# Linear attention feeding a top-1 mixture of experts on one core: a head pair per load, tiles of two token chunks, and weight casts four pieces behind their loads

## The chip, the cores and the metric

The kernel runs on one core of a Trainium2 chip. The metric is the device time of one execution in microseconds. The kernel before was run three times: 467.87, 472.14 and 472.62 us, median 472.14. The profiled execution took 468.79 us.

In profiles PE is TensorE (PEld its weight load), DVE is VectorE, ACT is ScalarE, POOL is GpSimd and SP is the sync engine, which here only issues loads. Each engine works its own instructions off in order.

## The reference

```
q, k, v: (8 batches, 8 heads, 576 tokens, 64) float32
kv  = einsum('bhsd,bhse->bhde', k, v)
out = einsum('bhsd,bhde->bhse', q, kv)
rms = sqrt(mean(out * out, axis=-1) + 1e-6)
x   = (out / rms * g_norm)  as (4608 tokens, 512)
logits = x @ w_gate                       # 8 experts
e      = argmax(logits);  gate = softmax(logits)[e]
y      = gate * (relu(x @ w1[e]) @ w2[e]) # w1: 512x1024, w2: 1024x512, float32
```

Inputs are 28.3 MB of q, k and v, and 33.6 MB of expert weights.

## The kernel before

**Attention stage.** Batches are taken in pairs j (two batches r = 0, 1), and within a pair four head pairs i. A *tile* is one of q, k or v for one (j, i): 128 partitions by 18 runs of 64, 590 KB. Partitions 0 to 63 hold batch r = 0, partitions 64 to 127 batch r = 1, and each half is loaded by a DMA of its own (L186, two DMAs of 64 partitions for a tile, issued by SP). A partition holds nine neighbouring tokens of two heads, so each contiguous run in HBM is 2304 bytes. There are four buffers for k, four for v and three for q.

For each tile triple, `kv_slice` (L218) accumulates k and v products in PSUM, nine chunks of tokens, in 64x64 quarters of the array. `t_slice` (L202) transposes q, and ACT copies the result (L206). After four head pairs `fold` (L237) multiplies kv by an identity and by the gate weights, so that the attention output and the logits come from one product. `o_tile` (L262) then makes 128 tokens for all heads: matmuls into PSUM, ACT squares (L270), DVE sums (L274), ACT takes the root (L276, L277), DVE scales into `xrow` (L279) and into `lhat` (L283). Two PSUM buffers alternate. Nine o_tiles make one j. `route` computes the expert, the gate and each token's slot, and POOL scatters each o_tile's rows to a table `x_slots` in HBM (L343), nine scatters in a row for j = 0, 1, 2 and three times three for j = 3.

**Weights.** A *piece* is 512 KB: one quarter of w1 (L163) or w2 (L167) of one expert, numbered 0 to 63 here. SP loads it into one of three float32 buffers `wst`, and a cast (L172) writes it to float16 and frees the buffer. Pieces 0 to 23 are interleaved with the attention loads, two for each tile triple, and cast on POOL. The others are cast on DVE.

**Expert stage.** For each of eight experts POOL gathers 640 rows (L405), PE transposes them (L424), DVE copies (L425), PE multiplies by w1 (L443), ACT applies relu (L451), PE multiplies by w2 (L455), DVE scales (L460) and POOL scatters to the output (L463). One more tile of 128 rows serves an expert with more than 640 tokens; its weights are gathered by POOL (L548, L554).

The order of the instructions on an engine is set by a scheduler when the kernel is built: it starts from program order and moves instructions where it expects their operands early. So casts stand in DVE's order far from where the program names them.

Of the kernel before, what the change touches and what calls it, by code (L numbers as in the profile page):

```python
# [11 lines left out]
F32 = mybir.dt.float32  # L12
F16 = mybir.dt.float16
# [9 lines left out]
B, H, S, DH = 8, 8, 576, 64  # L23
# [19 lines left out]
def kernel(  # L43
# [30 lines left out]
    for j in range(4):  # L74
        for t in range(9):
            tok[:, j, t] = (2 * j + ar // 64) * S + 9 * (ar % 64) + t

# [8 lines left out]
        "pcol": arf[:, None],  # L86
        "w1off": arf[:, None] + 128.0 * np.arange(4, dtype=np.float32)[None, :],
        "w2off": arf[:, None] + 128.0 * np.arange(8, dtype=np.float32)[None, :],
# [34 lines left out]
    wgt = P_const.tile([128, 4, 8], F32, tag="wgt")  # L123
    nc.scalar.dma_start(wgt, moe_w_gate.rearrange("(t p) j -> p t j", p=128))
    epsb = P_const.tile([128, 1], F32, tag="epsb")
# [28 lines left out]

    def w_chunk(e, n, pool, bufs, cast):
        if n == 0:
            w_tiles[e] = (
                pool.tile([128, 4, F], F16, tag="w1e", bufs=bufs, name=f"w1e{e}"),
                pool.tile([128, 8, D], F16, tag="w2e", bufs=bufs, name=f"w2e{e}"),
            )  # L160
        st = P_wa.tile([128, F], F32, tag="wst", bufs=3, name=f"wst{e}_{n}")
        if n < 4:
            nc.sync.dma_start(st, moe_w1[e, 128 * n : 128 * n + 128, :])  # L163
            dst = w_tiles[e][0][:, n, :]
        else:
            m = 2 * (n - 4)
            nc.sync.dma_start(  # L167
                st.rearrange("p (t d) -> p t d", t=2),
                moe_w2[e, 128 * m : 128 * m + 256, :].rearrange("(t p) d -> p t d", p=128),
            )  # L170
            dst = w_tiles[e][1][:, m : m + 2, :].rearrange("p t d -> p (t d)")
        cast(dst, st)  # L172

    with (
# [4 lines left out]

        def load_pair(j, i):  # L180
            for n, src in (("k", k), ("v", v), ("q", q)):
                t = PA.tile(
                    [128, 18, 64], F32, tag=f"m{n}", bufs=3 if n == "q" else 4, name=f"m{n}{j}{i}"
                )
                for r in range(2):
                    nc.sync.dma_start(  # L186
                        t[64 * r : 64 * r + 64].rearrange("p (h c) d -> p h (c d)", h=2),
                        src[2 * j + r, 2 * i : 2 * i + 2].rearrange("h (p c) d -> p h (c d)", c=9),
                    )
                main[n, j, i] = t  # L190

        qT, kvps, kvx = {}, {}, {}

        def t_slice(j, i):
            if i == 0:
                qT[j] = PA.tile([128, 36, 128], F32, tag="qT", bufs=2, name=f"qT{j}")
            src = main["q", j, i].rearrange("p b d -> p (b d)")
            for u in range(3):
                ps = PSA.tile([128, 3, 128], F32, tag="T", bufs=2)
                for c in range(3):  # L200
                    m = 3 * u + c
# [3 lines left out]
                m = 9 * i + 3 * u  # L205
                nc.scalar.copy(qT[j][:, m : m + 3, :], ps)  # L206

        def kv_slice(j, i):
            if i == 0:
                kvps[j] = [  # L210
                    PSA.tile([128, 4, 64], F32, tag=f"KV{r}", bufs=1, name=f"kvps{j}{r}")
                    for r in range(2)
                ]
            for c in range(9):
                for a in range(2):
                    for r in range(2):
                        rs_ = slice(64 * r, 64 * r + 64)
                        nc.tensor.matmul(  # L218
                            kvps[j][r][64 * a : 64 * a + 64, i, :],
                            main["v", j, i][rs_, 9 * a + c, :],  # L220
                            main["k", j, i][rs_, 9 * a + c, :],
                            start=(c == 0), stop=(c == 8),
                        )

        def fold(j):
            for r in range(2):
                z = PA.tile([128, 4, 64], F32, tag="z", bufs=2)
                nc.vector.tensor_copy(z, kvps[j][r])
                x = PA.tile([128, 4, 2, 72], F32, tag="kvx", bufs=4, name=f"kvx{j}{r}")
                pss = [  # L230
                    PSA.tile([128, 4, 72], F32, tag="T", bufs=2, name=f"fold{a}") for a in range(2)
                ]
                for i in range(4):
                    for a in range(2):
                        hs = slice(64 * a, 64 * a + 64)
                        for d in range(2):
                            nc.tensor.matmul(  # L237
                                pss[a][64 * d : 64 * d + 64, i, :], z[hs, i, :], fold_r[hs, i, :],
                                start=True, stop=True,
                            )  # L240
                for a in range(2):
                    nc.vector.tensor_copy(x[:, :, a, :], pss[a])
                kvx[2 * j + r] = x

        xrow, lhat = {}, {}

        def o_tile(j, t):
# [7 lines left out]
            ps = PSA.tile([128, 2, 512], F32, tag="O", bufs=2)  # L255
            for i in range(4):
                for a in range(2):
                    blk = 9 * (2 * i + a) + t
                    hs = slice(64 * (blk % 2), 64 * (blk % 2) + 64)
                    for r in range(2):  # L260
                        rs_ = slice(64 * r, 64 * r + 64)
                        nc.tensor.matmul(  # L262
                            ps[rs_, a, 72 * i : 72 * i + 72],
                            qT[j][hs, blk // 2, rs_],
                            kvx[2 * j + r][hs, i, a, :],
                            start=True, stop=True,
                        )
            pv = ps[:, :, 0:288].rearrange("p a (h c) -> p a h c", c=72)
# [10 lines left out]
            nc.vector.tensor_tensor(  # L279
                xr[:, 0:D].bitcast(F16).rearrange("p (h a d) -> p a h d", a=2, h=4),  # L280
                pv[:, :, :, 0:64], _bc(rs2, 3, 64), op=ALU.mult,
# [67 lines left out]

        w_order = [(e, n) for e in range(3) for n in range(8)]  # L350

        def w_some(n):
            for _ in range(min(n, len(w_order))):
                e, c = w_order.pop(0)
                w_chunk(e, c, P_wa, 3, nc.gpsimd.tensor_copy)

        for i in range(4):
            load_pair(0, i)
        o_of = {0: (0, 1), 1: (2, 3), 2: (4, 5), 3: (6, 7, 8)}
        for j in range(5):  # L360
            for i in range(4):
                if j < 4:
                    kv_slice(j, i)
                    t_slice(j, i)
                if j + 1 < 4:
                    load_pair(j + 1, i)
                w_some(2)
                if j > 0:
                    for t in o_of[i]:
                        o_tile(j - 1, t)  # L370
                        for t0, t1 in chunks[j - 1]:
                            if t + 1 == t1:
                                route(j - 1, t0, t1)
            if j < 4:
                fold(j)
        w_some(24)

    with (
# [41 lines left out]
        def xpose(xl, xsT, K):  # L420
            for k in range(K):
# [5 lines left out]
                )  # L427

        def ffn(K, xl, idv, w, views, tag=""):
            w1e, w2e = w  # L430
# [5 lines left out]
            for f in range(8):  # L436
# [127 lines left out]

        for n in range(8):
            w_chunk(3, n, PF, 3, nc.vector.tensor_copy)
        for e in range(E):
            if e + 1 < E:
                load_x(e + 1)
            slot_ids(e)  # L570
            if e == 1:
                tabs = dyn_tables()
            if 4 <= e + 3 < E:
                for n in range(8):
                    w_chunk(e + 3, n, PF if e + 3 < 6 else P_wa, 3, nc.vector.tensor_copy)
# [42 lines left out]
```

## Time and profile before

| | value |
|---|---|
| median of three runs | 472.14 us |
| profiled execution | 468.79 us |
| its span (first to last instruction) | 467.0 us |
| mean granted PE clock, share of full | 0.779 |
| PE, DVE, ACT, POOL busy | 68%, 36%, 24%, 35% of the span |
| moved by DMA | 83.80 MB, mean 179 GB/s |

Three parts follow each other: attention with loads (to about 180 us), attention's last tiles and routing (to 234 us), and the experts. A share of busy time over the whole span says little, since each part waits for something else. Read the stretches apart. The granted clock is that of PE: 0.50 is 1.2 GHz, 1.00 is 2.4 GHz.

### The profile page before, as it was taken

The numbers are of one execution on the slowest core, as the hardware profiler recorded it, in microseconds if no ns is written. First come the engines' busy times: TensorE is split into PE (matmuls) and PEld (weight loads), VectorE is DVE, ScalarE is ACT, GpSimd is POOL, SyncE is SP. The second block draws the span as 40 slices with busy tenths as digits, with TensorE's granted clock in tenths as the row PEclk, the third lists the DMA queues.
The fourth block names the chain that finished last, engine by engine and source line by source line (L and its number), as shares of the span: only waits on it lengthen the run. The fifth ranks groups of instructions, "written<-read, shape, count | busy, mean of one in ns | idle before, by whom it ended". The sixth has DMA issues, their size and how long they took to land. (4 is left out here: it accounts for less than half of the span.)

```text
span 467.0 us, 9241 instructions
## 1 busy us (share of the span) xinstructions
PE 315.7 (68%) x3782; PEld 221.1 (47%) x3782; DVE 166.5 (36%) x415; ACT 113.3 (24%) x299; POOL 163.2 (35%) x161
## 2 busy tenths in 40 slices
PE   2677766757675879343027965893759696969891
PEld 2576655656564667233014543361425354545550
DVE  2001624226322455266356634633302223232311
ACT  1211522115220345042102222040022131323330
POOL 3001111551107410714272450743753525252212
PEclk9999556557566568855556999796958999999997
DMA  8999999999999895301166897879461313131101
GB/s 200 241 243 264 255 253 246 269 268 237 231 217 245 231 266 183 124 25 54 49 209 210 292 349 257 313 267 268 128 95 56 102 34 113 36 131 45 62 34 74
DMA packets 37003, 83.80 MB, mean 179 GB/s; under 512 B 5981, under 2 KB 7262, under 8 KB 36960
## 3 DMA queue, kind: packets, MB, share of 16 engines
q1 hardware_dynamic: 27136, 61.88, 50.0%
q0 software_dynamic: 8704, 21.06, 14.8%
q8 instruction: 30, 0.49, 0.5%
q10 hardware_dynamic: 1120, 0.27, 0.3%
q14 instruction: 13, 0.11, 0.1%
HBM read 71.75 MB, written 15.50 MB: 187 GB/s over the span
## 5 line engine op out<-in xcount | busy, mean ns | idle before, releaser
L451 ACT ACTIVATE hT<-hp 128x320 f16<-128x320 f32 (+1 forms) x136 | 51.4, 427 | 172.1 <-PE hp L443 107.1
L443 PE MATMUL hp<-xsT,w1e 128*128 128x320 f16 x512 | 81.4, 315 | 15.9 <-ACT hT L451 10.3
L455 PE MATMUL yp<-w2e,hT 128*128 128x512 f16 x320 | 77.0, 400 | 15.8 <-DVE y L460 13.2
L262 PE MATMUL ps<-kvx,qT 64*64 64x72 f32 x1152 | 51.3, 307 | 41.5 <-DVE lhat L283 26.7
L463 POOL DMA_INDIRECT out_dram<-y,idv x41 | 42.5, 1036 | 98.8 <-DVE y L460 87.6
L218 PE MATMUL kvps<-mk,mv 64*64 64x64 f32 x1152 | 56.0, 292 | 28.2 <-issue 15.2
L443 PEld LDWEIGHTS <-w1e 128*128 128x128 f16 x512 | 52.0, 102 | 42.0 <-issue 20.7
L218 PEld LDWEIGHTS kvps<-mk,mv 64*64 64x64 f32 x1152 | 51.9, 197 | 31.5 <-issue 31.4
L262 PEld LDWEIGHTS ps<-kvx,qT 64*64 64x64 f32 x1152 | 41.7, 197 | 48.9 <-issue 43.7
L455 PEld LDWEIGHTS <-hT 128*128 128x128 f16 x328 | 33.3, 102 | 57.8 <-issue 21.1
L460 DVE TENSOR_SCALAR y<-yp,xl 128x512 f32<-128x512 f32 x41 | 30.7, 749 | 74.5 <-PE yp L455 72.6
L343 POOL DMA_INDIRECT x_slots<-xrow,posi x36 | 34.9, 970 | 53.3 <-DVE posi L327 23.7
L274 DVE TENSOR_REDUCE ms<-sq 128x8 f32<-128x512 f32 x36 | 24.6, 685 | 70.8 <-ACT sq L270 48.4
L405 POOL DMA_INDIRECT xl<-x_slots,xidx x40 | 42.7, 1068 | 14.8 <-issue 11.3
L270 ACT ACTIVATE sq<-ps 128x512 f32<-128x512 f32 x36 | 21.4, 597 | 96.0 <-PE ps L262 64.9
L202 PE MATMUL ps<-ctile,mq 128*128 128x128 f32 x144 | 34.8, 399 | 2.8 <-ACT qT L206 1.4
L206 ACT COPY qT<-ps 128x384 f32<-128x384 f32 x48 | 22.6, 478 | 49.0 <-PE ps L202 48.5
L424 PE MATMUL ps<-h,xl 128*128 128x128 f16 x164 | 16.2, 231 | 25.1 <-DMA xl<-x_slots,xidx 15.8
L172 POOL CAST w2e<-wst 128x1024 f16<-128x1024 f32 x12 | 12.5, 1044 | 57.2 <-DMA wst<-in_moe_w_dram 57.2
L172 POOL CAST w1e<-wst 128x1024 f16<-128x1024 f32 x12 | 12.3, 1042 | 56.0 <-DMA wst<-in_moe_w_dram 56.0
L202 PEld LDWEIGHTS ps<-ctile,mq 128*128 128x128 f32 x144 | 24.1, 202 | 9.9 <-ACT qT L206 6.3
L279 DVE TENSOR_TENSOR xrow<-ps,rs 128x512 f16<-128x512 f32 x36 | 24.7, 685 | 8.1 <-ACT rs L277 8.0
(86 smaller groups left out, 187.7 us busy)
## 6 DMA issues: line engine op xcount, KB each, us to landing
wst<-in_moe_w_dram SPq DMA_DIRECT2D x64, 512.0 KB
mk<-in_k_dram SPq DMA_DIRECT2D x32, 288.0 KB
mv<-in_v_dram SPq DMA_DIRECT2D x32, 288.0 KB
mq<-in_q_dram SPq DMA_DIRECT2D x32, 288.0 KB
out_dram<-y,idv POOLq DMA_INDIRECT x41
xl<-x_slots,xidx POOLq DMA_INDIRECT x40
x_slots<-xrow,posi POOLq DMA_INDIRECT x36
ctile<-c_all ACTq DMA_DIRECT2D x1, 133.0 KB
```

Of the source, the lines that this page charges most:

```text
L172: cast(dst, st)
L202: nc.tensor.transpose(ps[:, c, :], src[:, 128 * m : 128 * m + 128], cv["ident"])
L218: nc.tensor.matmul(kvps[j][r][64 * a : 64 * a + 64, i, :], main["v", j, i][rs_, 9 * a + c, :], main["k", j, i][rs_, 9 * a + c, :], start=( ...
L262: nc.tensor.matmul(ps[rs_, a, 72 * i : 72 * i + 72], qT[j][hs, blk // 2, rs_], kvx[2 * j + r][hs, i, a, :], start=True, stop=True,)
L279: nc.vector.tensor_tensor(xr[:, 0:D].bitcast(F16).rearrange("p (h a d) -> p a h d", a=2, h=4), pv[:, :, :, 0:64], _bc(rs2, 3, 64), op=ALU. ...
L343: nc.gpsimd.indirect_dma_start(out=xs_views[9 * j + t0 + t], out_offset=IndirectOffsetOnAxis(ap=posi[:, t : t + 1], axis=0), in_=xrow[j, ( ...
L405: nc.gpsimd.indirect_dma_start(out=xl[:, k, :], out_offset=None, in_=xs.ap(), in_offset=IndirectOffsetOnAxis(ap=xidx[:, e, k : k + 1], axi ...
L443: nc.tensor.matmul(hp[a], w1e[:, kk, f * 128 : (f + 1) * 128], xsT[:, kk, s : s + step], start=(kk == 0), stop=(kk == 3),)
L451: nc.scalar.activation(hT[:, f, s : s + step], hp[a], ACTF.Relu)
L455: nc.tensor.matmul(yp, hT[:, f, k * 128 : (k + 1) * 128], w2e[:, f, :], start=(f == 0), stop=(f == 7),)
L460: nc.vector.tensor_scalar(y, yp, xl[:, k, D : D + 2].bitcast(F32), None, op0=ALU.mult)
L463: nc.gpsimd.indirect_dma_start(out=views[k], out_offset=IndirectOffsetOnAxis(ap=idv[:, k : k + 1], axis=0), in_=y, in_offset=None, bounds_ ...
```

## The change

A tile is now one batch b and a half u of its heads: two head pairs, each of which fills the 128 partitions (head a = 0 on partitions 0 to 63, head a = 1 on 64 to 127). It still has 590 KB and runs of 2304 bytes, but one DMA of 128 partitions loads it (L203). There are still 16 triples, now by (b, u), with the same number of buffers. The fold is done for each batch. An o_tile takes 64 + 64 tokens from two token chunks of one batch; only t = 4 joins the last chunks of the two batches. The row's head order changes to (a, h), and the tables `w1off`, the gate weights' load and the w1 pieces' rows are permuted to match.

A piece is loaded by `w_load` into one of four buffers, and `w_cast` casts the piece that was loaded four pieces earlier. In attention `w_step` does one piece for each triple from b = 1 on, instead of two. The remaining pieces are named inside the experts' loop over f.

```diff
@@ weights
-        st = P_wa.tile([128, F], F32, tag="wst", bufs=3, name=f"wst{e}_{n}")
+        st = P_wa.tile([128, F], F32, tag="wst", bufs=4, name=f"wst{e}_{n}")
         if n < 4:
-            nc.sync.dma_start(st, moe_w1[e, 128 * n : 128 * n + 128, :])
+            r0 = 128 * (2 * (n % 2) + n // 2)
+            nc.sync.dma_start(st, moe_w1[e, r0 : r0 + 128, :])
...
-        cast(dst, st)
+        w_staged.append((dst, st))
+
+    def w_cast(engine):
+        if w_staged:
+            engine.tensor_copy(*w_staged.pop(0))
@@ loads
-        def load_pair(j, i):
+        def load(b, u):
             for n, src in (("k", k), ("v", v), ("q", q)):
                 t = PA.tile(
-                    [128, 18, 64], F32, tag=f"m{n}", bufs=3 if n == "q" else 4, name=f"m{n}{j}{i}"
+                    [128, 2, 576], F32, tag=f"m{n}", bufs=3 if n == "q" else 4, name=f"m{n}{b}{u}"
                 )
-                for r in range(2):
-                    nc.sync.dma_start(
-                        t[64 * r : 64 * r + 64].rearrange("p (h c) d -> p h (c d)", h=2),
-                        src[2 * j + r, 2 * i : 2 * i + 2].rearrange("h (p c) d -> p h (c d)", c=9),
-                    )
+                nc.sync.dma_start(
+                    t,
+                    src[b, 4 * u : 4 * u + 4].rearrange("(i a) (p c) d -> (a p) i (c d)", a=2, c=9),
+                )
@@ order of the program
-        for j in range(5):
-            for i in range(4):
-                if j < 4:
-                    kv_slice(j, i)
-                    t_slice(j, i)
-                if j + 1 < 4:
-                    load_pair(j + 1, i)
-                w_some(2)
-                if j > 0:
-                    for t in o_of[i]:
-                        o_tile(j - 1, t)
...
-            if j < 4:
-                fold(j)
-        w_some(24)
+        def w_step(n=1):
+            for _ in range(n):
+                if len(w_staged) == 4:
+                    w_cast(nc.gpsimd)
+                w_load(P_wa, 3)
+
+        for b in range(B + 1):
+            j = (b - 1) // 2
+            for u in range(2):
+                if b < B:
+                    kv_slice(b, u)
+                    t_slice(b, u)
+                if b + 2 < B:
+                    load(b + 2, u)
+                if b > 0:
+                    w_step()
+                    for i in (2 * u, 2 * u + 1):
+                        t = 5 * ((b - 1) % 2) + i
+                        o_tile(j, t)
...
+            if b < B:
+                fold(b)
+                if b % 2 == 1:
+                    j = b // 2
+                    o_tile(j, 4)
@@ in ffn, after each f
+                if not tag:
+                    w_cast(nc.vector)
+                    w_next()
```

The first place is SP's queue around the last attention loads (names: `mk33` is k of j = 3, i = 3; `mk71` is k of b = 7, u = 1; `wst2_4` is piece 4 of expert 2). Before:

```order
L163 DMA wst2_2_1251<-in_moe_w1_dram 128x1024
L163 DMA wst2_3_1254<-in_moe_w1_dram 128x1024
L186 DMA mk32_1361<-in_k_dram 64x2x576 x2
L186 DMA mv32_1364<-in_v_dram 64x2x576 x2
L186 DMA mq32_1367<-in_q_dram 64x2x576 x2
L167 DMA wst2_4_1370<-in_moe_w2_dram 128x2x512
L167 DMA wst2_5_1373<-in_moe_w2_dram 128x2x512
L186 DMA mk33_1479<-in_k_dram 64x2x576 x2
L186 DMA mv33_1482<-in_v_dram 64x2x576 x2
L186 DMA mq33_1485<-in_q_dram 64x2x576 x2
L167 DMA wst2_6_1488<-in_moe_w2_dram 128x2x512
```

and now:

```order
L203 DMA mk70_1497<-in_k_dram 128x2x576
L203 DMA mv70_1499<-in_v_dram 128x2x576
L203 DMA mq70_1501<-in_q_dram 128x2x576
L177 DMA wst1_0_1506<-in_moe_w1_dram 128x1024
L203 DMA mk71_1613<-in_k_dram 128x2x576
L203 DMA mv71_1615<-in_v_dram 128x2x576
L203 DMA mq71_1617<-in_q_dram 128x2x576
L177 DMA wst1_1_1620<-in_moe_w1_dram 128x1024
L177 DMA wst1_2_1780<-in_moe_w1_dram 128x1024
L177 DMA wst1_3_1887<-in_moe_w1_dram 128x1024
```

Ahead of the last q tile stood 22 pieces (to piece 5 of expert 2); now nine do (to piece 0 of expert 1), and each tile is one row where two DMAs were.

The second place is DVE's queue where the routing of j = 2 ends and the last batch's o_tiles begin (`kvx` is the folded product that o_tile uses). Before:

```order
L327 CAST posi_2144<-pos_2142 128x9
L242 COPY kvx30_2168<-fold0_2169 128x4x72
L242 COPY kvx30_2168<-fold1_2170 128x4x72
L242 COPY kvx31_2191<-fold0_2192 128x4x72
L242 COPY kvx31_2191<-fold1_2193 128x4x72
L274 TENSOR_REDUCE ms_2233<-sq_2231 128x8
L274 TENSOR_REDUCE ms_2259<-sq_2257 128x8
L279 TENSOR_TENSOR xrow30_2213<-ps_2214,rs_2235 128x2x4x64
```

and now:

```order
L262 COPY kvx6_1995<-fold0_1996 128x2x144
L352 CAST posi_1970<-pos_1968 128x9
L262 COPY kvx6_1995<-fold1_1997 128x2x144
L190 CAST w2e1_1505<-wst1_4_2071 128x1024
L190 CAST w2e1_1505<-wst1_5_2179 128x1024
L299 TENSOR_REDUCE ms_2094<-sq_2092 128x8
L190 CAST w2e1_1505<-wst1_6_2320 128x1024
L299 TENSOR_REDUCE ms_2120<-sq_2118 128x8
L304 TENSOR_TENSOR xrow30_2074<-ps_2075,rs_2096 128x512
```

Before, no cast stood on DVE ahead of the last route; now twelve do (pieces 12 to 23), between the last o_tiles. POOL casts pieces 0 to 11. In the experts' part 25 casts stood ahead of the first y of the second expert, and 27 stand there now.

## Rows read from the trace of the kernel before

**Rows 1.** Busy time by stretch: stretch, length, busy of five engines, clock, DMA share, GB/s.

```profile
50.00:75.00 25.00, 17.08 (x374) 15.53 (x367) 11.98 (x29) 9.15 (x26) 4.17 (x4) 0.50 1.06 253
200.00:225.00 25.00, 9.45 (x232) 8.42 (x233) 16.22 (x56) 9.20 (x28) 5.91 (x7) 0.50 0.11 38
```

**Rows 2.** The same view, three short stretches.

```profile
14.00:18.00 4.00, 2.70 (x56) 2.56 (x58) 0.00 (x0) 0.48 (x1) 0.00 (x0) 1.00 1.06 240
94.00:98.00 4.00, 1.74 (x12) 0.88 (x11) 0.48 (x1) 0.60 (x1) 3.08 (x5) 0.50 1.03 347
300.00:304.00 4.00, 2.92 (x30) 1.88 (x28) 3.46 (x8) 0.44 (x1) 3.17 (x3) 1.00 1.02 396
```

**Rows 3.** Timeline of SP's queue: start, length, engine, line, operation, tile, count.

```profile
33.63 1.61 SPq L163 DMA_DIRECT2D wst<-in_moe_w_dram  x2
...
43.09 3.23 SPq L163 DMA_DIRECT2D wst<-in_moe_w_dram  x2
...
166.26 1.68 SPq L186 DMA_DIRECT2D mq<-in_q_dram  x2
...
251.39 6.13 SPq L163 DMA_DIRECT2D wst<-in_moe_w_dram  x4
...
312.26 5.93 SPq L167 DMA_DIRECT2D wst<-in_moe_w_dram  x4
```

**Rows 4.** Timeline of POOL and ACT around scatters; brackets: idle before, and releaser.

```profile
143.76 0.98 POOL L343 DMA_INDIRECT x_slots<-xrow,posi  x1 [0.17 <-issue]
...
152.64 0.96 POOL L343 DMA_INDIRECT x_slots<-xrow,posi  x1 [0.30 <-issue]
...
155.25 1.10 ACT L270 ACTIVATE sq<-ps 128x512 f32<-128x512 f32 x2 [14.88 <-remote]
```

**Rows 5.** Timeline of POOL, end of routing: the first gather of the experts' rows.

```profile
234.32 1.44 POOL L405 DMA_INDIRECT xl<-x_slots,xidx  x1 [2.83 <-DVE w1e L172]
```

**Rows 6.** Timeline of PE, four kinds of work at 1.2 GHz, and the first matmuls.

```profile
7.80 3.45 PE L218 MATMUL kvps<-mk,mv 64*64 64x64 f32 x72 [7.80 <-DMA mv<-in_v_dram]
...
37.29 1.70 PE L237 MATMUL fold<-fold_r,z 64*64 64x72 f32 x32
...
126.22 3.31 PE L218 MATMUL kvps<-mk,mv 64*64 64x64 f32 x72
...
176.50 2.37 PE L202 MATMUL ps<-ctile,mq 128*128 128x128 f32 x9
...
202.47 2.20 PE L262 MATMUL ps<-kvx,qT 64*64 64x72 f32 x64 [9.81 <-DVE lhat L283]
```

**Rows 7.** Timeline of PE, the same work at 2.4 GHz.

```profile
183.02 1.90 PE L218 MATMUL kvps<-mk,mv 64*64 64x64 f32 x72
184.85 0.87 PE L202 MATMUL ps<-ctile,mq 128*128 128x128 f32 x6
185.97 0.55 PE L202 MATMUL ps<-ctile,mq 128*128 128x128 f32 x3 [0.24 <-ACT qT L206]
...
187.08 0.92 PE L237 MATMUL fold<-fold_r,z 64*64 64x72 f32 x32 [0.29 <-ACT qT L206]
...
190.03 1.32 PE L262 MATMUL ps<-kvx,qT 64*64 64x72 f32 x48 [0.38 <-DVE kvx L242]
```

**Rows 8.** Groups by line: casts on DVE, busy us and mean ns.

```profile
L172 DVE CAST w2e<-wst 128x1024 f16<-128x1024 f32 x20 | 14.0, 701 | 17.3 <-DMA wst<-in_moe_w_dram 15.6 <-issue 1.7
```

**Rows 9.** Timeline of POOL's gathers in the experts' stage.

```profile
299.79 1.25 POOL L405 DMA_INDIRECT xl<-x_slots,xidx  x1 [0.31 <-issue]
301.35 1.02 POOL L463 DMA_INDIRECT out_dram<-y,idv  x1 [0.30 <-DVE y L460]
```

**Rows 10.** Who waited for whom: us in total, times, longest.

```profile
PE yp L455 <- DVE y L460: 13.2, 3, 7.7
```

**Rows 11.** Timeline of POOL: the first casts of pieces.

```profile
43.12 1.04 POOL L172 CAST w1e<-wst 128x1024 f16<-128x1024 f32 x1 [37.95 <-DMA wst<-in_moe_w_dram]
...
55.52 1.04 POOL L172 CAST w1e<-wst 128x1024 f16<-128x1024 f32 x1 [8.51 <-DMA wst<-in_moe_w_dram]
```

More of the change, by code (lines that the diff above doesn't have):

```diff
@@ L123 @@
     wgt = P_const.tile([128, 4, 8], F32, tag="wgt")
-    nc.scalar.dma_start(wgt, moe_w_gate.rearrange("(t p) j -> p t j", p=128))
+    wg_src = moe_w_gate.rearrange("(x y z e) j -> y e x z j", x=2, y=2, z=2)
+    for y in range(2):
+        for x in range(2):
+            nc.scalar.dma_start(wgt[64 * y : 64 * y + 64, 2 * x : 2 * x + 2, :], wg_src[y, :, x])
     epsb = P_const.tile([128, 1], F32, tag="epsb")
@@ L153, with w_load @@
     w_tiles = {}
-    def w_chunk(e, n, pool, bufs, cast):
+    w_todo = [(e, n) for e in range(E) for n in range(8)]
+    w_staged = []
+    def w_load(pool, bufs):
+        if not w_todo:
+            return
+        e, n = w_todo.pop(0)
         if n == 0:
@@ L204, in t_slice, with kv_slice @@
                     )
[L205 to L212, printed above, removed]
+                m = 9 * u + 3 * g
+                nc.scalar.copy(qT[b][:, m : m + 3, :], ps)
+        def kv_slice(b, u):
+            if u == 0:
+                kvps[b] = [
+                    PSA.tile([128, 2, 64], F32, tag=f"KV{a}", bufs=1, name=f"kvps{b}{a}")
+                    for a in range(2)
@@ L213, in kv_slice @@
                 ]
             for c in range(9):
-                for a in range(2):
-                    for r in range(2):
-                        rs_ = slice(64 * r, 64 * r + 64)
+                cs = slice(64 * c, 64 * c + 64)
+                for y in range(2):
+                    for a in range(2):
+                        hs = slice(64 * a, 64 * a + 64)
                         nc.tensor.matmul(
-                            kvps[j][r][64 * a : 64 * a + 64, i, :],
-                            main["v", j, i][rs_, 9 * a + c, :],
-                            main["k", j, i][rs_, 9 * a + c, :],
+                            kvps[b][a][64 * y : 64 * y + 64, u, :],
+                            main["v", b, u][hs, y, cs],
+                            main["k", b, u][hs, y, cs],
@@ L222, in kv_slice, with fold @@
                             start=(c == 0), stop=(c == 8),
                         )
[L225 to L232, printed above, removed]
-                for i in range(4):
-                    for a in range(2):
-                        hs = slice(64 * a, 64 * a + 64)
+        def fold(b):
+            z = PA.tile([128, 2, 2, 64], F32, tag="z", bufs=2)
+            for a in range(2):
+                nc.vector.tensor_copy(z[:, a], kvps[b][a])
+            x = PA.tile([128, 2, 2, 2, 72], F32, tag="kvx", bufs=4, name=f"kvx{b}")
+            pss = [
+                PSA.tile([128, 2, 2, 72], F32, tag="T", bufs=2, name=f"fold{y}") for y in range(2)
+            ]
+            for u in range(2):
+                for a in range(2):
+                    for y in range(2):
+                        ys = slice(64 * y, 64 * y + 64)
@@ L243, in fold @@
-                kvx[2 * j + r] = x
+            for y in range(2):
+                nc.vector.tensor_copy(x[:, :, y], pss[y])
+            kvx[b] = x
         xrow, lhat = {}, {}
```

84 lines of the change are left out of this document (44 added, 40 removed).

## The prediction

> **What bounds the kernel now.** I read the busy time by stretch first, since the three parts have different limits. In the attention part the DMA engines are full (share 1.06) and PE works 17.1 of 25 us at 1.2 GHz; in 200 to 225 us the same engines move 38 GB/s and DVE, with 16.2 of 25 us, is the busiest [rows 1]. So the first part waits for transfers, and the second for a chain of small steps. The three short stretches then show that a full queue does not always move the same: one with attention loads alone moves 240 GB/s, one with weight pieces 347, one with pieces, gathers and output rows 396 [rows 2]. The attention loads are the 64-partition DMAs; the pieces fill 128 partitions.
>
> SP's queue gives the end of the first part: the last q tile is issued at 166.3 us [rows 3]. Until then 47 of the 48 tiles (27.7 MB), 22 pieces of 0.524 MB (11.5 MB) and 18 scatters of 128 rows of 1032 bytes (2.4 MB) have been issued: 41.6 MB in 165.5 us, or 251 GB/s. The first gather of the experts comes at 234.3 us [rows 5], 68 us after that issue, and the span ends at 467.0, 232.7 us later. These three lengths (166.3, 68.0, 232.7) are my terms.
>
> **First term: until the last q tile is issued.** The order shows nine pieces ahead of it where 22 stood, so 34.8 MB remain. At 251 GB/s this takes 139 us; at the 347 of the pieces 100; at 396, 88. The new tile has runs of 2304 bytes in 128 partitions, two to a partition; the w2 pieces have runs of 2048 bytes, two to a partition, also 128 partitions, and they were among what moved at 396 [rows 2]. The run length before is the same 2304 bytes, so what differs is the half of the partitions, and I take 347 rather than 251. The Trainium skill (SBUF — State Buffer, Door 1: The DMA port swizzle) says that partitions 0 to 63 reach only eight of sixteen ports, with asymptotes of 218 and 436 GB/s for half and all, and that two half transfers don't add up. The trace agrees in direction, with 240 beside 347, though 240 is above the page's half. As an estimate from that page, 34.8 MB at 436 GB/s would be 80 us, which leaves the sum as it is, because PE comes next.
>
> For what is late next is PE. The last q tile waits for a buffer, that is for the transposes of tile (6, 0). By the order PE has then done 13.2 kv tiles, 13 transposed tiles, six folds and 23 o_tiles. At 1.2 GHz one costs 3.31, 2.37, 1.70 and 1.10 us (half of the row's two o_tiles) [rows 6]: 43.7 + 30.8 + 10.2 + 25.3 = 110 us. At 2.4 GHz it is 1.90, 1.67 (from 184.85 to the end of the second row), 0.92 and 0.88 us (two thirds of the row) [rows 7]: 25.1 + 21.7 + 5.5 + 20.2 = 72.5 us. To both I add the start, 7.8 us [rows 6], and two scatter blocks: while POOL issues nine scatters PE nearly stops, and ACT goes on at 155.25, after the last of them [rows 4]. From 143.76 that is 11.5 us, of which PE works about 2; two times 9.5 is 19 us. Before, full queues covered these blocks; with faster loads they are bare. PE's path is then 137 us at the low clock and 99 at the high one. The clock rose between 176.5 and 183.0 us [rows 6, 7], where kv tiles and transposes followed each other almost without a wait, so denser work should raise it part of the time. Between 100 (loads) or 99 (PE, high) and 137 (PE, low) I take the middle, **120 us**; the range keeps 100 and 139.
>
> **Second term: from there to the first gather.** The work left is the same as before: three kv tiles and transposes, two folds, 13 o_tiles, four routes and 18 scatters. New are twelve casts on DVE, 0.70 us each [rows 8], 8.4 us in all. DVE had 8.8 us idle in the 25 of [rows 1] and the other half of this part is no denser, so I count them at nothing; the whole 8.4 if that idle time is only waiting inside the chain. Their pieces, 9 to 23, are 7.9 MB, 23 us at 347 GB/s within 68 us in which the queue was nearly empty. POOL is slower beside a cast: a gather took 1.25 us where 1.02 is usual [rows 9]; 0.23 for 18 scatters is 4.1 us at most. The Trainium skill (SBUF — State Buffer, Who interferes with whom) speaks against this move: a DVE copy or cast in a two-port mode and GpSimd lock each other out for a whole instruction. By that rule twelve scatters could each wait 0.70 us, 8.4 us together instead of 4.1; the row shows a third of it. In the other direction the last tile lands sooner: a load took 9.5 us to its cast in a full queue [rows 3, 11], and 251/347 of that saves 2.6. So **68 us**, from 65 to 80.
>
> **Third term: the experts.** SP issues the last 32 pieces in 66.8 us [rows 3], 2.09 us each. Four buffers instead of three let one more be under way, and PE's waits for y that stood behind casts, 13.2 us [rows 10], could go entirely. But the order puts two more casts ahead of the second expert's first y, 4.2 us at 2.09. Between -13.2 and +4.2 I take -5, near the middle: **227.7 us**. The number of pieces left for this part is the same (36 or 37), so there is no bill for those that left the first part: they go into the empty stretch.
>
> **Edits at nothing:** the gate weights' load in four DMAs on ACT's queue, wanted by the first fold only at 37 us; 16 half-sized copies of kvps for eight whole ones; the permuted tables; 48 load issues instead of 96 on SP, which isn't the bound.
>
> **The sum** is 120 + 68 + 227.7 = 415.7 us of span; with the 1.8 us that the execution's 468.8 lies above its span, **418 us**. That execution is 3.3 us below the median of the runs and within their spread, so I leave it at that.
>
> **The rivals.**
> - *The first part keeps its pace.* Either half-partition DMAs weren't the cause of 240, or PE stays at 1.2 GHz: 139 or 137 us lead to the same. For it: PE was at 1.2 GHz through most of this part, and the chain of an o_tile (ACT, DVE, ACT, DVE) leaves it gaps. Against it: the 347. Time: 138 + 68 + 227.7 + 1.8 = 436 us. Chance 0.22.
> - *Everything gives.* PE reaches 2.4 GHz early, loads set 100 us, and the experts' waits for y vanish: 100 + 68 + 219.5 + 1.8 = 389 us. For it: at 183 us one tile triple passed in 3.5 us. Against it: dense work needs loads ahead of it, and scatters break it. Chance 0.12.
> - *Slower: the hand-over of buffers on DVE.* A piece is issued only when the cast four places earlier has run, and these casts now stand between the last o_tiles. If each group of four costs a whole trip from issue to cast, three trips lengthen the second term, and nine (36 pieces) replace the 83.9 us from the first gather to SP's last piece (318.2) [rows 3, 5]. The time is 120 + 68 + 3x + (232.7 - 83.9) + 9x + 1.8. With the second trip in the rows, 43.09 to 55.52, x is 12.4 [rows 3, 11] and the time 487; with the first, 9.5, it is 453. It decides against the change from x = 11.2 on. Against it: both trips ran in a full queue of other loads, which isn't there later. Chance 0.05.
>
> **How the numbers follow.** My forecast, 405 to 430 us with 418 in it, has 0.58; the named rivals 0.39, and 0.03 is left for what I don't see. The range goes from 388 to 450: it takes in the fast rival, the slow pace with the second term's upper bound of 80 (448), and leaves out the hand-over. About 1% is what a measurement of this kernel can tell from no change. Faster by more: forecast, both rivals of the first part and most of the rest, 0.92. Within 1%, 0.03. Slower, 0.05.
>
> **What would show it.** The stretch of attention loads alone at 300 GB/s or more, where 240 stood, shows the first step; a value near 245 refutes it. SP's last q issue near 120 us shows the first term, and the granted clock there (above 0.5 in part of the stretches) the reason for its middle. The first gather 68 us later shows that casts on DVE are covered; waits of DVE's sums or of casts for pieces before the last route would show that they are not. PE's waits for y below 13 us show the third term. I would be wrong most if PE, not the queue, had been setting the first part's pace, or if DVE stood still at pieces in the middle of the last routes.

## The result, and the profile after

The changed kernel takes 428.8 us (median of four runs, 425.4 to 434.0), the kernel before on the same chip 470.0 (464.9 to 472.6). The ratio is 0.917, 95% interval 0.902 to 0.932. Medians and ranges here and below are of all runs of a kernel, while a ratio leaves out runs that lie over 1.5% above the fastest of their kernel. The profiled execution took 425.42 us with a span of 423.6. Forecast were 418 us and a range of 388 to 450.

Busy time by stretch of the changed kernel (columns as in [rows 1, 2]: stretch, length, busy of PE, PE's weight loads, DVE, ACT, POOL, granted clock, DMA share, GB/s):

```profile
14.00:18.00 4.00, 4.00 (x81) 3.48 (x80) 0.49 (x2) 0.95 (x2) 0.00 (x0) 1.00 1.03 380
...
34.00:38.00 4.00, 1.91 (x60) 1.64 (x57) 2.02 (x7) 0.30 (x2) 0.00 (x0) 0.79 1.04 410
...
50.00:75.00 25.00, 15.76 (x281) 11.82 (x281) 7.89 (x30) 4.93 (x15) 10.86 (x11) 0.62 0.64 229
...
102.00:110.00 8.00, 4.43 (x63) 2.96 (x61) 0.69 (x1) 1.08 (x2) 6.17 (x7) 0.71 0.81 253
...
175.00:200.00 25.00, 2.12 (x52) 1.72 (x47) 11.34 (x46) 2.99 (x11) 10.54 (x10) 0.50 0.28 94
```

Read the first row beside that of [rows 2]: the same kind of stretch, attention loads alone and a full queue, moves 380 GB/s where it moved 240, and 410 at 34 us. The third row answers to the first of [rows 1]: from 50 us on the queue is no longer full, 0.64 where 1.06 stood. So the wait for transfers has gone from most of the first part, and something else sets its pace. SP's own waits (engine, line, for whom: us in total, times, longest) name it: the loads wait for the transposes that free the buffers of q.

```profile
SPq L203 <- PE ps L219: 62.2, 10, 12.4
```

The fourth row of the stretches shows one thing that holds PE up: in 8 us in which POOL issues seven scatters, DVE completes one operation and PE 63 matmuls.

The same block on the timelines of POOL, PE, DVE and SP (start, length, engine, line, operation, tile, count; in brackets the idle time before, and who ended it):

```profile
99.17 0.98 POOL L368 DMA_INDIRECT x_slots<-xrow,posi  x1 [8.47 <-DVE posi L352]
...
104.78 0.34 PE L287 MATMUL ps<-kvx,qT 64*64 64x72 f32 x3 [0.85 <-issue]
106.21 0.30 PE L287 MATMUL ps<-kvx,qT 64*64 64x72 f32 x3 [1.08 <-issue]
...
108.31 0.69 DVE L299 TENSOR_REDUCE ms<-sq 128x8 f32<-128x512 f32 x1 [8.96 <-issue]
...
109.33 0.96 POOL L368 DMA_INDIRECT x_slots<-xrow,posi  x1 [0.30 <-issue]
...
123.61 0.37 SPq L203 DMA_DIRECT2D mq<-in_q_dram  x1
...
194.19 1.56 POOL L433 DMA_INDIRECT xl<-x_slots,xidx  x1 [3.18 <-DVE d_gt L520]
```

"Issue" is a wait for nothing that the profile shows. PE gets a few matmuls done between scatters (three at 104.78, three at 106.21), DVE stands for 8.96 us. The last two rows give the lengths: the last q tile at 123.6 us (166.3 in [rows 3]), the first gather at 194.2 (234.3 in [rows 5]), the end at 423.6.

| | before | forecast | after |
|---|---|---|---|
| to the last q's issue | 166.3 | 120 | 123.6 |
| from there to the first gather | 68.0 | 68 | 70.6 |
| from there to the end | 232.7 | 227.7 | 229.4 |

Nearly the whole gain, 42.7 of the 43.4 us by which the span is shorter, lies in the first length.

PE at the start, as in [rows 6], and at 117 us:

```profile
6.89 2.20 PE L236 MATMUL kvps<-mk,mv 64*64 64x64 f32 x72 [6.89 <-DMA mv<-in_v_dram]
9.02 2.37 PE L219 MATMUL ps<-ctile,mq 128*128 128x128 f32 x9
...
117.89 0.99 PE L236 MATMUL kvps<-mk,mv 64*64 64x64 f32 x52
```

The transposes cost what they did (2.37 us); the kv tile takes 2.20, where it took 3.45 at this place before and I had priced it at 3.31 us at 1.2 GHz and 1.90 at 2.4. The prediction had not seen that.

Waits, in the same columns as SP's above, the first the answer to [rows 10]:

```profile
PE yp L493 <- DVE y L498: 8.5, 3, 5.1
...
DVE w2e L190 <- DMA wst<-in_moe_w_dram: 7.1, 5, 1.8
```

### The profile page after: what moved, and what is told of

Its sections match the earlier page's. It is cut to its first block, busy times and chain, and to the rows that moved or that the text cites. A ratio compares the mean times of both kernels' runs of the same rounds, so it can differ in the third digit from the quotient of the medians.

```text
span 423.6 us, 9162 instructions
## 1 busy us (share of the span) xinstructions
PE 288.4 (68%) x3782; PEld 190.1 (45%) x3782; DVE 168.1 (40%) x435; ACT 111.3 (26%) x299; POOL 151.3 (36%) x149
## 4 chain that ended last, share of the span: by engine, by line
issue 17%; PE 17%; POOL 6%; DMA 4%; DVE 3%; another core or an unknown queue 3%; ACT 1%; POOLq 1%
PE hp L478 8%; PE yp L493 8%; POOL out_dram L501 4%; POOL xl L433 2%; DMA xl<-x_slots,xidx 2%; DMA wst<-in_moe_w_dram 2%; PE ps L452 1%; DVE y L498 1%; ACT hT L486 1%; DMA out_dram<-y,idv 1%; DVE xsT L453 1%; DVE w2e L190 1%; POOLq L646 0%; POOL xl L578 0%
## 5 line engine op out<-in xcount | busy, mean ns | idle before, releaser
L478 PE MATMUL hp<-xsT,w1e 128*128 128x320 f16 x512 | 80.4, 313 | 15.3 <-ACT hT L486 10.6
L493 PE MATMUL yp<-w2e,hT 128*128 128x512 f16 x320 | 78.7, 406 | 12.6 <-DVE y L498 8.5
L287 PE MATMUL ps<-kvx,qT 64*64 64x72 f32 x1152 | 45.6, 279 | 25.6 <-DVE lhat L308 10.7
L287 PEld LDWEIGHTS ps<-kvx,qT 64*64 64x64 f32 x1152 | 35.1, 172 | 36.5 <-issue 29.9
L236 PE MATMUL kvps<-mk,mv 64*64 64x64 f32 x1152 | 30.2, 246 | 19.7 <-issue 10.3
L236 PEld LDWEIGHTS kvps<-mk,mv 64*64 64x64 f32 x1152 | 26.3, 157 | 22.5 <-issue 22.0
L223 ACT COPY qT<-ps 128x384 f32<-128x384 f32 x48 | 22.4, 478 | 45.6 <-PE ps L219 43.8
L190 POOL CAST w1e<-wst 128x1024 f16<-128x1024 f32 x8 | 8.3, 1042 | 59.9 <-DMA wst<-in_moe_w_dram 59.9
L219 PEld LDWEIGHTS ps<-ctile,mq 128*128 128x128 f32 x144 | 20.5, 179 | 17.0 <-ACT qT L223 9.3
L452 PEld LDWEIGHTS <-xl 128*128 128x128 f16 x164 | 12.0, 102 | 30.6 <-issue 24.2
```

The source lines that it names most:

```text
L219: nc.tensor.transpose(ps[:, c, :], src[:, 128 * m : 128 * m + 128], cv["ident"])
L236: nc.tensor.matmul(kvps[b][a][64 * y : 64 * y + 64, u, :], main["v", b, u][hs, y, cs], main["k", b, u][hs, y, cs], start=(c == 0), stop=(c ...
L287: nc.tensor.matmul(ps[64 * r : 64 * r + 64, y, o0 : o0 + 72], qT[b][hs, blk // 2, 64 * a : 64 * a + 64], kvx[b][hs, u, y, a, :], start=Tru ...
L452: nc.tensor.transpose(ps[:, c, :], xl[:, k, c * 128 : (c + 1) * 128].bitcast(F16), ident16)
L478: nc.tensor.matmul(hp[a], w1e[:, kk, f * 128 : (f + 1) * 128], xsT[:, kk, s : s + step], start=(kk == 0), stop=(kk == 3),)
L493: nc.tensor.matmul(yp, hT[:, f, k * 128 : (k + 1) * 128], w2e[:, f, :], start=(f == 0), stop=(f == 7),)
```

## Experiments

The runs fell on chips of two kinds. The kernel before took 461 to 476 us on the chips of c_after, c_after2 and of the result above, and 421 to 428 us on those of the first four runs and of the last two. So a ratio to the kernel before is always that of the same chip, and absolute times are compared within one kind only. Times that were expected for the other kind than the run fell on can't be read.

**e1_halves: the loads' width undone.** The edit changes nothing else, but with it the scheduler also reorders the kv matmuls; the next run has nearly that order with wide loads.

```diff
-                nc.sync.dma_start(
-                    t,
-                    src[b, 4 * u : 4 * u + 4].rearrange("(i a) (p c) d -> (a p) i (c d)", a=2, c=9),
-                )
+                pairs = src[b, 4 * u : 4 * u + 4].rearrange("(i a) (p c) d -> a p i (c d)", a=2, c=9)
+                for a in range(2):
+                    nc.sync.dma_start(t[64 * a : 64 * a + 64], pairs[a])
```

> The changed kernel with each q, k or v tile loaded by two DMAs of 64 partitions instead of one of 128; bytes, tiles, the weights' places and lags stay. The program then also puts the kv matmuls of one partition half ahead of the other's, 13 and 13, as the kernel before had them. Width theory (the prediction's): the stretches of attention loads alone, 14 to 38 us, fall from 380 to 413 GB/s to about 240; the last q tile is issued at 34.8 MB / 251 GB/s = about 139 us instead of 123.6, and the time is about 444 us (438 to 455). Pace theory (PE and the scatters set the first part in both kernels): the rate may fall, but the last q stays within 4 us of 123.6 and the time within 424 to 433.

415.6 us (413.1 to 418.3) beside 425.2 of the kernel before, ratio 0.975 [0.970, 0.981]. Its rows: a short stretch, a long one, the last q and the first gather.

```profile
14.00:18.00 4.00, 2.71 (x27) 1.99 (x27) 0.00 (x0) 1.43 (x3) 0.00 (x0) 1.00 1.05 236
...
50.00:75.00 25.00, 20.79 (x383) 18.46 (x381) 11.96 (x37) 8.73 (x23) 2.18 (x3) 1.00 1.03 240
...
144.11 1.25 SPq L205 DMA_DIRECT2D mq<-in_q_dram  x2
...
206.41 1.53 POOL L432 DMA_INDIRECT xl<-x_slots,xidx  x1 [5.10 <-DVE d_gt L519]
```

The rate is back at 236 to 240 GB/s with a full queue (1.03), and the last q is issued at 144, close to the 139 expected. How much time that is, the comparison with the next run says.

**e5_kv_halves: wide loads, kv matmuls one partition half after the other**, nearly as in e1_halves.

```diff
-            for c in range(9):
-                cs = slice(64 * c, 64 * c + 64)
-                for y in range(2):
-                    for a in range(2):
-                        hs = slice(64 * a, 64 * a + 64)
+            for a in range(2):
+                hs = slice(64 * a, 64 * a + 64)
+                for c in range(9):
+                    cs = slice(64 * c, 64 * c + 64)
+                    for y in range(2):
```

> The changed kernel with only the order of the kv matmuls changed: 18 of one partition half, then 18 of the other, where they went round the four quarters; loads stay 128 partitions wide. Order theory: a kv tile (72 records) takes about 3.45 us at the start instead of 2.20, and about 1.9 at 2.4 GHz instead of 1.3 to 1.4; PE's busy time in kv goes from 30 to about 56 us. If PE sets the first part, 13 tiles by 1 us make the last q 10 to 16 us later and the time about 440; if scatters and the o_tile's chain set it, the time stays within 425 to 432. Rival: the kv tiles got faster because of something else (the loads' width, what else is on the queue), and their time stays at 2.20 us.

390.4 us (389.8 to 391.8), ratio 0.919 [0.915, 0.924].

```profile
7.01 3.75 PE L236 MATMUL kvps<-mk,mv 64*64 64x64 f32 x72 [7.01 <-DMA mv<-in_v_dram]
...
14.00:18.00 4.00, 3.85 (x73) 3.76 (x74) 0.35 (x2) 0.00 (x0) 0.00 (x0) 1.00 1.05 413
...
98.00:106.00 8.00, 7.42 (x212) 6.46 (x205) 5.65 (x12) 5.23 (x15) 6.18 (x8) 0.88 0.97 301
...
110.11 0.37 SPq L203 DMA_DIRECT2D mq<-in_q_dram  x1
...
174.17 1.56 POOL L433 DMA_INDIRECT xl<-x_slots,xidx  x1 [3.05 <-DVE d_gt L520]
```

Three things follow. The width: beside e1_halves this kernel is 25.2 us faster, and the first length holds it (110.1 instead of 144.1; the other two are 64.1 and 62.3, 213.8 and 210.1). The order: the kv tile is back at 3.75 us, so the order of the quarters is what made it 2.20; yet the kernel is within 3 us of e4_spread below, which has the quick order, and its last q is issued no later (110.1 us beside 113.3). So most of that price seems to be covered on this chip; it is not shown alone, since the changed kernel itself was not run there. And the third row is a scatter block in which nothing stops: POOL is as busy as in the changed kernel's block (6.18 of 8 us), but PE does 212 matmuls instead of 63.

**e2_more_pieces: 24 pieces in the attention part.**

```diff
-                    w_step()
+                    w_step(2 if w_todo[0][0] < 2 else 1)
```

> The changed kernel with 24 weight pieces (as in the kernel before) instead of 16 in the attention part; 17 instead of 9 of them ahead of the last q tile, 4.2 MB more, and 8 casts that were DVE's become POOL's. If the queue sets the first part, 4.2 MB at 405 GB/s make the last q 10 us later and the time 435 to 440. If it does not (its share is 0.64 to 0.77 from 50 us on), the last q stays at 122 to 126 us and the time at 424 to 431; the eight casts that DVE loses may then give back up to 5.6 us.

384.1 us (383.6 to 386.3), ratio 0.905 [0.900, 0.910], on the chip of e1_halves and e5_kv_halves.

```profile
93.00:101.00 8.00, 8.00 (x192) 6.67 (x194) 3.23 (x8) 4.40 (x11) 6.16 (x7) 0.62 0.76 259
...
108.03 0.47 SPq L203 DMA_DIRECT2D mq<-in_q_dram  x1
...
169.12 1.18 POOL L433 DMA_INDIRECT xl<-x_slots,xidx  x1 [2.81 <-issue]
```

Eight pieces more ahead of the last q do not delay it: 108.0 us, sooner than the 110.1 and 113.3 of e5_kv_halves and e4_spread, which have nine. So with wide loads the queue does not set the first part on this chip, and there the fewer pieces ahead of the last q are not what the change gained by. The expected times (424 and up) were meant for the other kind of chip.

**e4_spread: one scatter to a chunk instead of nine in a row**, run on both kinds of chip. `put` issues one scatter; `put_one` is called at the end of each o_tile. Since rows now wait longer for their scatter, `xrow` also gets seven buffers instead of five.

```diff
             for t in range(T):
-                nc.gpsimd.indirect_dma_start(
...
+                if j < 3:
+                    rows.append((j, t0 + t, pos[:, t : t + 1]))
+                else:
+                    put(j, t0 + t, posi[:, t : t + 1])
...
+        def put_one(ms):
+            if rows:
+                j, t, pos = rows.pop(0)
+                at = PA.tile([128, 1], I32, tag="at", bufs=3)
+                nc.vector.scalar_tensor_tensor(
+                    out=at, in0=ms[:, 0:1], scalar=0.0, in1=pos, op0=ALU.mult, op1=ALU.add
+                )
+                put(j, t, at)
```

> The changed kernel with the nine scatters of a batch pair (pairs 0 to 2) issued one after each of the next nine token chunks, through a small DVE operation (27 of them, 0.15 us each) that makes the index wait for that chunk's sum; the last pair as it was. Block theory: nine scatters in a row stop PE, DVE and ACT for 9 to 10 us, and one by one they go beside the chain of a chunk: the two blocks ahead of the last q tile vanish, it is issued at 105 to 112 us instead of 123.6, the first gather is 3 to 10 us sooner relative to it, and the time is about 410 us (402 to 418). Rival: each scatter stops the other engines for its own 0.97 us wherever it stands, so that 27 of them cost the same 26 us, and the time stays within 424 to 432.

387.6 us (385.7 to 390.9), ratio 0.910 [0.905, 0.915]: where nothing stops at scatters it lies between e2 and e5. It was then run again beside the changed kernel.

> The changed kernel again, as the control beside the next run. Two of the chips used so far differ: on one the kernel before takes 425 us and PE goes on while POOL issues nine scatters, on the others 468 to 472 us and PE nearly stops. Where the kernel before takes 425, this takes 384 to 392 us; where it takes 468, 428 to 434. If the change's gain hung on the scatter blocks, the two ratios to the kernel before would differ by more than 0.02.

> The kernel with its scatters one to a chunk, again, beside the control on the same chip. Block theory: where PE nearly stops at nine scatters in a row, the two blocks ahead of the last q tile cost 2 times 9 us that the spread gives back, and the time is 12 to 22 us below the control's; where PE goes on, within 4 us of it. Rival: a scatter stops PE for its own time wherever it stands; then it is within 4 us of the control on either chip.

This time the kernel before took 470.4 us. The changed kernel took 435.6 (433.9 to 437.7), ratio 0.929 [0.922, 0.936]; with spread scatters it took 417.1 (413.8 to 422.3), ratio 0.883 [0.874, 0.891]. That is 18.5 us less by the medians and 21.6 by the ratios (0.046 of 470.4), in the expected 12 to 22, and the intervals don't meet. First the control's rows, then those of the spread kernel:

```profile
105.00:113.00 8.00, 4.54 (x64) 2.89 (x64) 0.69 (x1) 1.50 (x3) 6.08 (x7) 0.71 0.72 199
...
127.64 0.37 SPq L203 DMA_DIRECT2D mq<-in_q_dram  x1
...
198.61 1.56 POOL L433 DMA_INDIRECT xl<-x_slots,xidx  x1 [3.02 <-DVE d_gt L520]
```

```profile
102.00:110.00 8.00, 6.58 (x200) 5.12 (x195) 6.60 (x17) 3.84 (x12) 5.21 (x6) 1.00 1.00 344
...
112.99 0.37 SPq L203 DMA_DIRECT2D mq<-in_q_dram  x1
...
182.42 1.25 POOL L451 DMA_INDIRECT xl<-x_slots,xidx  x1 [2.62 <-DVE w1e L190]
```

With six scatters in the 8 us, 200 matmuls instead of 64, and the last q 14.7 us sooner: that is what the two blocks ahead of it cost, net of what spreading costs. The rival (a scatter stops the others for its own time wherever it stands) falls. With spread scatters the last q also comes at the same time on both kinds of chip (113.3 us in e4_spread, 113.0 here, one execution each), so up to there the blocks seem to be all that the kinds differ by.

**c_after and c_before: both kernels on a chip of the first kind.**

> The changed kernel unchanged, as the control for the experiments, which ran where the kernel before takes 425 us and not 470. If what the experiments did there is worth little (a kv order, spread scatters, more pieces: 390, 388 and 384 us beside 425), this one comes to 384 to 392 us, a ratio of 0.905 to 0.922. If the order of the kv matmuls costs 10 us or more, it comes to 380 or less; if spreading the scatters or the pieces' place gave 10 us, to 395 or more.

> The kernel before, unchanged, for its profile where it takes 425 us. Theory: the 45 us between 470 and 425 lie where POOL issues a run of indirect DMAs (scatter blocks, gathers): there PE, ACT and DVE stood still in one execution (nine scatters, 11.4 us, PE busy for about 2) and go on working in the other. Then attention loads alone still move 240 GB/s, and the last q tile comes 15 to 25 us sooner than at 166.3. Rival: the memory is faster there; then the rate is above 260 GB/s.

They fell on a chip where the kernel before takes 468.5 us, so the controls that the first four runs wanted are missing: the changed kernel itself was not run where the kernel before takes 425. It took 433.7 us, ratio 0.918 [0.907, 0.929], as in the result. The one profile of the kernel before (460.9 us) shows its block and its rate again:

```profile
14.00:18.00 4.00, 2.73 (x47) 2.36 (x47) 0.00 (x0) 0.76 (x2) 0.00 (x0) 1.00 1.06 243
...
87.00:95.00 8.00, 3.37 (x51) 2.10 (x52) 0.69 (x1) 0.60 (x1) 5.92 (x7) 0.63 1.04 322
...
137.86 10.39 SPq L163 DMA_DIRECT2D wst<-in_moe_w_dram  x2
...
158.97 1.91 SPq L186 DMA_DIRECT2D mq<-in_q_dram  x2
```

The second row is the prediction's word "bare" in numbers: in the kernel before PE stops as well (51 matmuls), but the DMA share is 1.04 meanwhile, so the transfers that it waits for go on. In the rows of the changed kernel's blocks above it is 0.72 and 0.81. That a block costs the kernel before nothing is argued from this share and was not tested. For its second block it does not hold: in the third row SP needs 10.4 us to issue two pieces, because a buffer for them comes free only with casts that POOL has queued behind the scatters.

**e3_no_lag: each piece of the attention part cast right behind its load.**

```diff
-                if len(w_staged) == 4:
-                    w_cast(nc.gpsimd)
                 w_load(P_wa, 3)
+                w_cast(nc.gpsimd)
```

> The changed kernel with each weight piece of the attention part cast by POOL right behind its load's issue, instead of four pieces later (the experts' part as it was). POOL then waits for each piece as it lands, 3 to 6 us, with scatters queued behind the wait. If the lag matters, scatters and with them the last route come later, and the time is 5 to 15 us above the control's; if POOL has time enough (10.9 of 25 us busy at most), it is within 3 us of the control.

428.6 us (419.0 to 431.5), beside 433.7 (427.6 to 436.6) of c_after on the same chip. Its runs are too far apart for a ratio. The two ranges overlap, and the expected loss of 5 to 15 us is not there: the lag buys nothing that could be seen.

**e8_both_q4: spread scatters, 24 pieces and a fourth q buffer together** (the edits of e4_spread and e2_more_pieces, and `bufs=4` for q).

> The changed kernel with three edits together: scatters spread one to a chunk, 24 pieces instead of 16 in the attention part, and four q buffers instead of three. SP waited 34 to 68 us for PE to free q buffers, so the loads then run further ahead; if the queue or its buffers limited the first part, the last q comes 8 us sooner and the time is 372 to 380 us where the kernel before takes 425. If PE and the chain of the o_tile set it, 381 to 388.

408.1 us (406.5 to 413.6) beside 468.5, ratio 0.869 [0.859, 0.878], on the chip of c_after. It beats the changed kernel by about 5%. The interval meets that of e4_spread2 (0.874 to 0.891, another chip), so what the pieces and the buffer add to the spread stays open.

**e1_halves2 and e5_kv_halves2: width and order once more.**

> The changed kernel with two 64-partition loads for one of 128, again. Where PE went on beside the scatters, it took 415.6 us beside 390.4 of the kernel with wide loads and nearly the same kv order: 25 us for the width alone. Where PE stops at scatters and the kernel before takes about 470 and the changed one 429 to 436: if the width is worth the same 25 us, 453 to 462 (ratio to the kernel before 0.965 to 0.985); if full queues cover the scatter blocks again, so that less of the width's price shows, 440 to 450 (0.935 to 0.955).

> The changed kernel with the kv matmuls one partition half after the other, again, beside e1_halves2, which differs from it by the loads' width alone. Where the kernel before takes about 470 us and the changed one 0.917 to 0.929 of it: if kv's order is on the path (13 tiles by about 1 us ahead of the last q), a ratio of 0.935 to 0.955; if the o_tile's chain and the scatter blocks set the first part, within 0.01 of 0.92. Where the kernel before takes 425, 390 as measured.

Again a chip of the second kind (the kernel before 423.3 us): 419.8 us, ratio 0.989 [0.979, 0.998], and 391.7, ratio 0.924 [0.917, 0.931]. The width is worth 28.2 us here, 25.2 the first time. That is most of what the change is worth on such chips: with loads of half the width and all the rest of the change, e1_halves gains 9.6 and e1_halves2 3.5 us over the kernel before. What the width and the kv order are worth on a chip where scatters stop PE was not measured.

## Why the prediction was right, and where it was not

**The first step, shown.** In the stretch from 14 to 18 us loads of 64 partitions move 236 to 243 GB/s in four profiles of two kernels, loads of 128 partitions 380 to 417 in ten of six. I had taken 347 from the weight pieces, too low, and the stretch was not one of pieces alone: 0.60 of its 1.39 MB went through POOL's queue (q0), which was issuing scatters there. For 94 to 98 us of the kernel before, by queue (packets, MB, share of 16 engines):

```profile
q1 hardware_dynamic: 298, 0.77, 55.0%
q0 software_dynamic: 217, 0.60, 45.8%
```

It did no harm, since PE came next. That splitting the loads lowers the rate is shown by e1_halves beside e5_kv_halves, which has nearly the same kv order: 236 GB/s beside 413. Whether it is the half of the partitions or the smaller DMA (288 KB instead of 576) no run separates; the DMA share, 1.05 in both, speaks against gaps between the DMAs. The Trainium skill gives 218 and 436 GB/s (SBUF — State Buffer, Door 1: The DMA port swizzle) and says that two transfers of a half don't add up (SBUF — State Buffer, "Can I just issue two DMAs to hit both halves?"). The runs agree on the last point, with 236 for two halves that stand next to each other in the queue; the measured pair is closer together than the page's.

**The first term, 123.6 for 120, right in sum from misjudged parts.** The mean of the prices at the two clocks was meant to stand for the mixture. By the groups of the changed kernel, and of c_before for the kv tile,

```profile
L287 PE MATMUL ps<-kvx,qT 64*64 64x72 f32 x1152 | 45.6, 279 | 25.6 <-DVE lhat L308 10.7 <-issue 10.5 <-DVE xrow L363 2.6
L219 PE MATMUL ps<-ctile,mq 128*128 128x128 f32 x144 | 34.2, 366 | 9.7 <-ACT qT L223 7.3 <-issue 1.9 <-DVE kvx L262 0.3
L236 PE MATMUL kvps<-mk,mv 64*64 64x64 f32 x1152 | 30.2, 246 | 19.7 <-issue 10.3 <-DMA mv<-in_v_dram 9.3
...
L256 PE MATMUL fold<-fold_r,z 64*64 64x72 f32 x256 | 14.3, 300 | 0.8 <-issue 0.8
```

```profile
L218 PE MATMUL kvps<-mk,mv 64*64 64x64 f32 x1152 | 57.2, 289 | 27.1 <-issue 14.3 <-DMA mv<-in_v_dram 12.7
```

(busy us, mean ns of one, then the idle time before them) a kv tile took 30.2 / 16 = 1.9 us, nine transposes 2.1, a fold 1.8, an o_tile 45.6 / 36 = 1.27. Times 13.2, 13, 6 and 23 that is 93 us. Neighbouring records overlap, though, and PE was busy for 82.9 us of this length, less than the 91 in the middle of my 72.5 and 110:

```profile
0.00:123.61 123.61, 82.89 (x2021) 66.75 (x2025) 47.88 (x144) 41.17 (x108) 31.41 (x33) 0.81 0.80 286
```

The kv term came out at 25 us, the very end that I had for 2.4 GHz, though the clock was there only part of the time (granted 0.81 over this length, 0.62 from 50 to 75 us): the matmuls had become cheaper by their order, 30.2 us in all where c_before has 57.2. The scatter blocks were priced too high as well: two times 9.5 us rested on PE working "about 2" of the 11.5 us, and the row of that stretch of the kernel before has 5.94:

```profile
143.76:155.25 11.49, 5.94 (x85) 4.12 (x88) 0.92 (x2) 0.00 (x0) 9.35 (x10) 0.53 0.87 239
```

By e4_spread2 the two blocks cost 14.7 us, not 19. So where I had 91 + 8 at the start + 19 = 118, rounded to 120, it was 83 + 7 + 15 = 105, and some 19 us are waits that I had put at nothing. That these errors nearly cancelled is luck. That the blocks would be bare was right; that full queues covered them before holds for the first block and not for the second (c_before above).

**The second term, 70.6 for 68.** The twelve casts were nearly covered: no cast on DVE waited more than 1.8 us for its piece in the profiled execution, and e2_more_pieces, with four casts there instead of twelve, needs 61.1 us for this length beside 62.2 (e4_spread, 175.43 - 113.26) and 64.1 (e5_kv_halves) on the same chip, 1 to 3 us for eight casts of 0.7, from one execution each. A scatter beside a cast took 1.22 us instead of 0.96:

```profile
147.41 1.22 POOL L368 DMA_INDIRECT x_slots<-xrow,posi  x1 [0.30 <-issue]
147.82 0.69 DVE L190 CAST w2e<-wst 128x1024 f16<-128x1024 f32 x1
148.93 0.96 POOL L368 DMA_INDIRECT x_slots<-xrow,posi  x1 [0.30 <-issue]
```

The Trainium skill's rule (SBUF — State Buffer, Who interferes with whom) that cast and scatter shut each other out for a whole instruction would make it up to 0.70 us; the trace shows 0.26, and [rows 9] had 0.23. That is not a third of the lock, as the prediction read it, for the two meet only in part: here the scatter ends 0.12 us after the cast, in [rows 9] 0.36 us of the cast were left when the gather began, and a scatter of e5_kv_halves that starts with a cast (149.30) takes 1.47 us. Where a cast on DVE meets three on POOL, in e2_more_pieces, the trace agrees with the rule in full: DVE's cast lasts until POOL's are done, 3.35 us instead of 0.69.

```profile
134.00 3.00 POOL L190 CAST w1e<-wst 128x1024 f16<-128x1024 f32 x3
134.20 3.35 DVE L190 CAST w2e<-wst 128x1024 f16<-128x1024 f32 x1
```

**The third term, 229.4 for 227.7.** PE's waits for y fell from 13.2 to 8.5 us; 4.7 went where 5 was booked. But other executions on chips of this kind have 233.5 us (c_after2, 432.1 - 198.61) with the change and 231.4 (c_before, 459.1 - 227.67) without it, so that this part became shorter is not shown.

**The rivals.** "Keeps its pace" fails with the rates. "Everything gives" fails on PE's path: the queue stood at 0.64. The hand-over on DVE fails too: groups of four did not cost a trip each, for no cast on DVE waited longer than 1.8 us for its piece (6.5 in c_after and 5.6 in c_after2, one each and in the experts' part).

**What stays open.** Why the kinds of chip differ, and how much the changed kernel gains over the kernel before where nothing stops (e5_kv_halves, which differs by the kv order alone, has 0.919 and 0.924 there). The kernel before is some 45 us faster there too; no profile of it from such a chip exists, so where it gains them, and what its own blocks cost it, is not known.

## What to carry to other kernels

Fill all 128 partitions with each load: a full DMA queue says that something waits for transfers, not that the transfers are as fast as they can be, so compare GB/s between stretches of the same share. When a full queue goes, look at what it covered; here it was two blocks of scatters, 14.7 us on a chip where scatters stop PE, which one small dependency per scatter removed. And take the price of a group of small matmuls from the order in which they will stand, not from the shape alone.

## What the runs showed of the hardware

**Quarters of the array.** 72 records of 64x64 matmuls (two to a matmul) took 2.20 us when consecutive ones went round the four quarters, and 3.75 us when 18 of one partition half came before 18 of the other, at the same place in the program and both with a granted clock of 1.00 in that stretch. The transposes beside them (2.37 us at 9.02) had the price that [rows 6] shows at 0.50, so at the start of a program the granted clock did not tell the price.

**Indirect DMAs and the other engines.** On some chips PE, DVE and ACT nearly stop while POOL issues indirect DMAs in a row, and on others they don't, with the same 0.96 us for a scatter (63 matmuls and one DVE operation in 8 us in the changed kernel on the one, 212 and 12 in e5_kv_halves on the other). It is not only the attention part, and not the kernel: e4_spread ran on both kinds. In the 15 us in which POOL issues the twelve gathers of the extra tile's weights, it has this row on the second kind of chip,

```profile
248.00:263.00 15.00, 8.01 (x51) 4.79 (x49) 3.78 (x7) 3.83 (x11) 11.48 (x12) 0.84 1.00 237
```

and this one on the first:

```profile
254.00:269.00 15.00, 4.19 (x23) 2.30 (x23) 3.47 (x6) 1.90 (x5) 11.34 (x13) 0.75 1.05 238
```

From the first gather to the end it needs 213.7 us (389.1 - 175.43) on the one and 234.4 (416.8 - 182.42) on the other. Of what the engines wait then, the profile shows only "issue" and, for ACT, a wait for something outside the core's view; the cause was not tried.
